# Queries first, scores ahead of states, set 2 held back, and identity matmuls in TensorE's first waits

## The chip, the cores and the metric

The kernel runs on one core of one Trainium2 chip. The metric is the device time of one execution in microseconds (us), as the median of several runs. An execution's profile has a span, from the first to the last instruction, and the execution's own time beside it.

## The reference

Decayed linear attention feeds a two-layer feed-forward block. B, H, S, D are 4, 8, 768, 64; the feed-forward widths are 512 and 2048.

```
Dmask = where(rel >= 0, lam ** rel, 0)            # rel = i - j within a block of 64
for each block b of 64 positions:
    intra = ((q_b @ k_b.T) * Dmask) @ v_b
    inter = (q_b * lam ** (pos + 1)) @ kv_state
    attn[b] = intra + inter
    kv_state = lam ** 64 * kv_state + (k_b * lam ** (63 - pos)).T @ v_b
x = attn with heads side by side                  # 3072 x 512
h = x @ w_in                                      # 3072 x 2048
out = (h * sigmoid(h)) @ w_out                    # 3072 x 512
```

## The kernel before

Positions are taken in units of 128, 24 units in all. Two units make a set, and there are 12 sets. The first four hold units 0 and 1 of one batch entry, interleaved by position; the other eight hold one unit of two batch entries. A set is loaded as three float32 tiles `raw` (k, q, v; `load_set`, L349 and L351), 0.5 MB each, on SyncE's (SP's) DMA queue, in the order k, q, v.

For one set: k and q are cast to bfloat16 (`kq`, L313 on ScalarE = ACT, L315 on VectorE = DVE); both are transposed (`kqT`), on TensorE (PE) by matmuls with the identity `ident` (L442) for the first four sets and by a DMA (L622) for the others; v is multiplied by a decay (`vd`). TensorE then makes the states (`d_ps`, L463 or L647) from k and `vd`, the scores (`st_ps`, L514 or L657) from `kqT`, and, after VectorE has masked the scores to `st`, the outputs (`x_ps`, L538 or L679), to which the carried state `xe` is added by a second group of matmuls (L543 or L687). `y`, `xf` and `yf` are the steps from `d_ps` to the next `xe`. VectorE multiplies `x_ps` by the queries' decay `lam_xe` while it moves it to `xt`, the transposed activations. `lam_xe` is made at the start on ACT from the integer row `row_i`.

The feed-forward part takes `xt` in groups: four of 256 columns (one for each of the first sets), then four of 512. `product1` (L830) multiplies by w_in into `h_ps`, ACT applies silu into `g` (L839), and `product2_plain` (L861) multiplies the first eight units by w_out into `o_ps`. The sixteen other units go through seven products for eight (a Strassen-Winograd scheme; `product2`, L1072, with sums `s` and `wsum`), and so does the last group's first product (`product1_spared`, L944). Results leave through `osb`.

The weights are loaded and cast to bfloat16 by GpSimd's (POOL's) DMA queue in quarters of 0.5 MB as they lie on chip (`load_w`; w_in is i0 to i3, w_out o0 to o3). `SEQUENCE` gives the order of sets and weights. Between them stand gates: `gated` lets POOL copy one element of a loaded `raw` tile, so that the weight loads behind it in POOL's queue are not issued before that load has landed. In before each gate waits for the k of the set named last.

The order of every engine is written out by `Planner.order`, a list scheduler: each task has a key, the engines that it may run on with an estimated time on each, its inputs and its buffers from small pools; the planner plays the tasks through and emits them in that order. TensorE runs its matmuls in program order, so one that waits holds all behind it.

Of the kernel before, what the change touches and what calls it, by code (L numbers as in the profile page):

```python
# [37 lines left out]
class Planner:  # L38

    LAT = {"PE": 0.23, "ACT": 0.06, "DVE": 0.06, "POOL": 0.08, "SP": 0.0}  # L40
    BEGIN = {"PE": 0.8, "ACT": 8.3, "DVE": 4.5, "POOL": 4.7, "SP": 0.8}
    FIRST, LAST, AHEAD = {"SP": 1.9, "ACT": 1.15, "POOL": 2.5}, 1.0, 0.75

    def __init__(self, pools):
        self.pools = {n: list(range(c)) for n, c in pools.items()}
        self.tasks = []

    def add(self, key, on, fn, deps=(), bufs=(), nbytes=0, kind=None, prior=(), late=0.0):
        key = key if isinstance(key, tuple) else (key,)
        t = Task(key, on, fn, deps, list(bufs) + [b.with_ for b in bufs if b.with_], nbytes, kind, prior, late)  # L50
        for b in t.bufs:
            b.left += 1
        self.tasks.append(t)
        return t

    def order(self):
# [14 lines left out]
        seq = 0  # L71
# [48 lines left out]
        while len(out) < len(self.tasks):  # L120
# [9 lines left out]
            for e in free:  # L130
# [8 lines left out]
                while ready[e]:  # L139
# [12 lines left out]
                    mine = now + t.on[e]  # L152
                    if any(max(free[o], now) + d < mine - 1e-9 for o, d in t.on.items() if o != e):
                        kept.append((key, i, t))
                        continue
# [4 lines left out]
                if took is None:  # L160
                    continue
# [5 lines left out]
                free[e] = now + t.on[e]  # L167
                heapq.heappush(events, free[e])
# [20 lines left out]
def kernel(  # L189
# [28 lines left out]
    SEQUENCE = "s0 i0 s1 i1 i2 s2 i3 o0 s3 o1 o2 o3 s4"  # L218
    POOLS = dict(bank=8, ra=3, rb=6, kq=3, kqT=3, vd=3, st=3, xe=6, xf=3, y=2, yf=2,
                 xt2=2, xt4=2, g=18, s=12, m=3, osb=3, one=3, two=4, att=6)  # L220
    BY_POOL, IN_BY_POOL, PLAIN, SPARED = (4,), (), 8, 1
    EARLY, PACE = 1.0, 1.0
    EAGER, CALM, ON = 8.0, 1.0, 6.0
# [36 lines left out]
    row_i = const.tile([128, U], mybir.dt.int32, name="row_i")  # L260
    nc.gpsimd.iota(row_i, pattern=[[1, U]], base=-64, channel_multiplier=0)
# [20 lines left out]
    pose_2 = const.tile([128, 2], F32, name="pose_2")  # L282
    for a in range(2):
        nc.vector.tensor_scalar(pose_2[:, a:a + 1], iota_2, -1.0, 64.0 - a, op0=AL.mult, op1=AL.add)
    pose = const.tile([128, 1], F32, name="pose")
    nc.vector.tensor_scalar(pose, iota_p, -1.0, 64.0, op0=AL.mult, op1=AL.add)
    row = const.tile([128, U], F32, name="row")
    nc.vector.tensor_copy(row, row_i)
# [6 lines left out]
    lam_v = const.tile([128, H], F32, name="lam_v")  # L295
    lam_xe = const.tile([128, NP, U], F32, name="lam_xe")
    lam_be = const.tile([128, NP], F32, name="lam_be")
    lam_v2 = const.tile([128, H, 2], F32, name="lam_v2")
    for a in range(2):
        nc.scalar.activation(lam_v2[:, :, a], log_all, AF.Exp, scale=pose_2[:, a:a + 1])  # L300
    nc.scalar.activation(lam_v, log_all, AF.Exp, scale=pose[:, 0:1])
    for a in range(NP):
        nc.scalar.activation(lam_xe[:, a, :], row, AF.Exp, scale=log_lam[:, a:a + 1])
# [26 lines left out]
    def gated(key, load, i, tile):  # L330
        pool_task(add(key, {"POOL": 0.15}, lambda e: nc.gpsimd.tensor_copy(gate[:, i:i + 1], tile()), deps=load,  # L331
                      prior=pool_last[-1:]))
# [3 lines left out]
    raw = {}  # L336

    def load_set(key, si):
        n, b = sets[si][0]
        nb = 2  # L340
        rs = [Buf("ra" if si in (0, 3) else "rb") for _ in range(3)]
# [4 lines left out]
        def go(e, i):  # L346
            if n < PAIRED:
                tile_of(rs[i], [128, H, 2, 64], F32, "raw")
                nc.sync.dma_start(out=rs[i].tile.rearrange("p h e d -> p h (e d)"), in_=x[i])  # L349
            else:  # L350
                nc.sync.dma_start(out=tile_of(rs[i], [128, 2 * H, 64], F32, "raw"), in_=x[i])  # L351

        for i in range(3):
            ts.append([add((key, i), {"SP": 0.55}, lambda e, i=i: go(e, i), bufs=[rs[i]], nbytes=0.524,
                           kind=WIDE if n < PAIRED else SMALL, late=0.3 if si < FRESH else 3.0)])
        raw[si] = rs, ts
# [3 lines left out]
    def load_w(key, what, j):  # L360
        def go(e):
            if what == "i":
                cs = slice(512 * j, 512 * j + 512)
                nc.gpsimd.dma_start(out=w_in_bf[:, :, cs], in_=w_in_r[:, :, cs])
            else:
# [3 lines left out]
        wload[what, j] = pool_task(add((key, 0), {"POOL": 0.8}, go, [], [], 1.0486,  # L369
                                       LARGE, prior=pool_last[-1:], late=1.0))  # L370

    last, unit = None, None
    for m, x in enumerate(SEQUENCE.split() + [f"s{i}" for i in range(len(sets))]):
        j = int(x[1:])
        if x[0] == "s":
            if j not in raw:
                load_set(m - 100, j)
                unit = j
        else:
            if last != unit:  # L380
                rs, loads = raw[unit]
                gated((m - 100, -1), loads[0], unit, lambda b=rs[0]: b.tile[:, 0, 0, 0:1] if len(b.tile.shape) == 4 else b.tile[:, 0, 0:1])
                last = unit
            load_w(m - 100, x[0], j)
# [25 lines left out]
    def key_of(si):  # L410
        u = rank[sets[si][0]]
        return u - 4.0 if sets[si][0][0] == 0 else u - LEAD

    def prepare_2(o, rs, lk, lq, lv):
# [5 lines left out]
        def cast(e, i, a):  # L420
            copy(e, o.kq_of()[:, i, :, a], rs[i].tile[:, :, a, :].rearrange("p (m h) d -> p m h d", h=2))

        o.ck = [[add((s - 1.0, i), {"DVE": 0.43, "ACT": 0.63}, lambda e, i=i, a=a: cast(e, i, a), deps=(lk, lq)[i],
                     bufs=[rs[i], o.kq]) for a in range(2)] for i in range(2)]
# [7 lines left out]
        o.cv = [add((s - 0.8, 0), {"DVE": 0.7}, lambda e, a=a: scale_v(e, a), deps=lv, bufs=[rs[2], o.vd]) for a in range(2)]  # L432
# [19 lines left out]
    def first_2(o):  # L452
# [13 lines left out]
        td = add((s - 0.6, 0), {"PE": 0.45}, states, deps=o.cv + o.ck[0], bufs=d_ps + [o.kq, o.vd])  # L466
        after("b", td)
# [13 lines left out]
        def blocks(xe, i, src, t, buf):  # L481
            def go(e, r):
                if xe.tile is None:
# [6 lines left out]
        t0 = add((s - 0.9, 3), {"DVE": 0.42}, lambda e: tt(e, small(xf), d_ps[0].tile, rate, AL.mult), deps=[td], bufs=[d_ps[0], xf])  # L490
        o.xe_ready = blocks(o.xe_in, 0, lambda: xf.tile, t0, xf)
        t1 = add((s - 0.9, 4), {"DVE": 0.42}, lambda e: tt(e, small(y), d_ps[1].tile, xf.tile, AL.add), deps=[td, t0],
                 bufs=[d_ps[1], xf, y])
        t2 = add((s - 0.9, 5), {"DVE": 0.42, "POOL": 0.7}, lambda e: tt(e, xf_of(), y.tile, rate, AL.mult), deps=[t1], bufs=[y, xf_n])
        xf_t.append(t2)
        xe_t += blocks(xe_n, b0 % 2, xf_of, t2, xf_n)

# [6 lines left out]
        o.st_of = st_of  # L504
        deps = [t for t in o.turned]
        o.masked = []
        for g in range(2):
# [11 lines left out]
            for p in range(2):  # L519
# [5 lines left out]
                o.masked.append(add((s - 0.9, 0), {"DVE": 0.69}, mask, deps=[ts], bufs=[st_ps[g][p], o.st2[p]]))  # L525
        after("m", o.masked)

    def second_2(o):
# [21 lines left out]
        for c in range(2):  # L550
            def evac(e, c=c):
                tl = tile_of(xt[gi], [128, KI, 256], BF16, "xt")
                dst = tl[:, :, 128 * c:128 * c + 128].rearrange("p m (c e) -> p m e c", e=2)
                tt(e, dst, x_ps[c].tile, lam_xe.rearrange("p m (c e) -> p m e c", e=2), AL.mult)

            xt_done[gi].append(add((s - 0.9, 6), {"DVE": 0.7}, evac, deps=[(t0, t1)[c]], bufs=[x_ps[c], xt[gi]]))

    def prepare(si):
# [7 lines left out]
        o.kq, o.kqT, o.vd, o.st = Buf("kq"), Buf("kqT"), Buf("vd"), Buf("st")  # L566
# [6 lines left out]
        def kq_of():  # L573
            return tile_of(o.kq, [128, nb, 2, NP, 2, 64], BF16, "kq")

        def kqT_of():
            return tile_of(o.kqT, [128, nb, 2, NP, U], BF16, "kqT")
# [9 lines left out]
        def cast(e, j, i):  # L587
            src = rs[i].tile[:, j * H:j * H + H, :].rearrange("p (m h) d -> p m h d", h=2)
            dst = kq_of()[:, j, i]
            copy(e, dst, src)  # L590

        ck = [[add((s - 1.0, i), {"DVE": 0.43, "ACT": 0.63}, lambda e, j=j, i=i: cast(e, j, i), deps=(lk, lq)[i],
                   bufs=[rs[i], o.kq]) for i in range(2)] for j in range(nb)]
        after("k", [t for ts in ck for t in ts])
# [4 lines left out]
        cv = [add((s - 0.8, 0), {"DVE": 0.7} if si < FRESH else {"POOL": 1.25, "DVE": 0.7}, lambda e, j=j: scale_v(e, j),  # L599
# [5 lines left out]
        if si < TURNED:  # L605
            for j in range(nb):
                bank = Bank(fills=False)

                def turn(e, j=j, bank=bank):
                    t = tile_of(bank, [128, 2, NP, U], BF16, "tr")  # L610
                    for i in range(2):
                        for m in range(NP):
                            nc.tensor.transpose(t[:, i, m, :], kq_of()[:, j, i, m], ident)

                tr = add((s - 0.7, j), {"PE": 0.46}, turn, deps=ck[j], bufs=[bank, o.kq])
                for i in range(2):
                    o.turned.append(add((s - 1.0, 2), {"DVE": 0.43, "ACT": 0.6},
                                        lambda e, j=j, i=i, bank=bank: copy(e, kqT_of()[:, j, i], bank.tile[:, i]),
                                        deps=[tr], bufs=[bank, o.kqT]))
        else:  # L620
            def dma_turn(e):
                nc.sync.dma_start_transpose(kqT_of().rearrange("p b i m s -> p (b i m) s"),  # L622
                                            kq_of().rearrange("p b i m h d -> p (b i m h d)"))
# [4 lines left out]
    def first_part(o):  # L628
# [12 lines left out]
        def states(e):  # L641
            for j in range(nb):
                for m in range(NP):
                    for c in halves_of_d:
                        r = halves[c]
                        for p, rp in enumerate(halves):
                            nc.tensor.matmul(d_of(c)[rp, j, m, :], lhsT=o.kq_of()[r, j, 0, m, p, :],  # L647
# [3 lines left out]
        def scores(e):  # L651
            for j in range(nb):
                for m in range(NP):
                    for p, rp in enumerate(halves):
                        t = tile_of(st_ps[p], [128, nb, NP, 64], F32, "st_ps")
                        for c, r in enumerate(halves):
                            nc.tensor.matmul(t[r, j, m, :], lhsT=o.kqT_of()[rp, j, 0, m, r], rhs=o.kqT_of()[rp, j, 1, m, r],  # L657
# [6 lines left out]
    def second_part(o):  # L664
# [18 lines left out]
        def inter(e):  # L683
            for c in range(2):
                for j in range(nb):
                    for m in range(NP):
                        nc.tensor.matmul(x_of(c)[:, j, m, :], lhsT=o.xe[c].tile[:, (bs[0] + j) % 2, m, :],  # L687
                                         rhs=o.kqT_of()[:, j, 1, m, halves[c]],
# [484 lines left out]
```

## Time and profile before

| | before |
|---|---|
| median of 3 runs | 207.87 us (207.69 to 208.84) |
| profiled execution | 207.82 us |
| its span | 206.1 us |
| TensorE busy | 187.0 us (91%), 2445 matmuls |
| VectorE busy | 134.8 us (65%) |
| ScalarE busy | 107.4 us (52%) |
| GpSimd busy | 52.4 us (25%) |
| mean DMA rate | 165 GB/s |

A line such as "L830 PE MATMUL h_ps<-xt,w_in_bf" names the line of the kernel, the engine, the operation and the tiles; "xt" is a tile's name, "x16" a count. All copies stand under L313, L315 or L317 and all two-input operations under L320, by engine, so there the tile names tell the step. An arrow in brackets names what ended the engine's idle time.

### The profile page before, as it was taken

The numbers are of one execution on the slowest core, as the hardware profiler recorded it, in microseconds if no ns is written. First come the engines' busy times: TensorE is split into PE (matmuls) and PEld (weight loads), VectorE is DVE, ScalarE is ACT, GpSimd is POOL, SyncE is SP. The second block draws the span as 40 slices with busy tenths as digits, with TensorE's granted clock in tenths as the row PEclk, the third lists the DMA queues.
The fourth block names the chain that finished last, engine by engine and source line by source line (L and its number), as shares of the span: only waits on it lengthen the run. The fifth ranks groups of instructions, "written<-read, shape, count | busy, mean of one in ns | idle before, by whom it ended". The sixth has DMA issues, their size and how long they took to land.

```text
span 206.1 us, 5719 instructions
## 1 busy us (share of the span) xinstructions
PE 187.0 (91%) x2445; PEld 132.9 (64%) x2464; DVE 134.8 (65%) x249; ACT 107.4 (52%) x195; POOL 52.4 (25%) x76
## 2 busy tenths in 40 slices
PE   0459399999999999999999999998999999999993
PEld 0347288786667565544578648474675778888882
DVE  6488632767950467716989953999758995665411
ACT  3637267874336453375734492745615453766420
POOL 7231400401130111222565013346003221222200
PEclk9999889999999999999999999999999999999999
DMA  3999999999999999999999999905101110102213
GB/s 99 292 253 260 228 222 265 235 199 214 228 238 249 156 216 231 238 219 195 263 213 234 203 213 240 244 7 117 39 3 54 51 54 0 54 0 102 88 52 118
DMA packets 88617, 33.92 MB, mean 165 GB/s; under 512 B 67088, under 2 KB 87568, under 8 KB 88592
## 3 DMA queue, kind: packets, MB, share of 16 engines
q1 hardware_dynamic: 79232, 23.60, 57.3%
q0 software_dynamic: 4224, 4.19, 12.2%
q10 hardware_dynamic: 5136, 5.77, 8.7%
q8 instruction: 19, 0.31, 0.7%
q14 instruction: 6, 0.05, 0.1%
HBM read 27.27 MB, written 6.29 MB: 163 GB/s over the span
## 4 chain that ended last, share of the span: by engine, by line
PE 82%; DMA 8%; DVE 7%; issue 1%; ACT 0%; POOL 0%; POOLq 0%; DVEq 0%
PE h_ps L830 31%; PE o_ps L1072 22%; PE o_ps L861 13%; PE h_ps L944 6%; DMA w_in_bf<-in_moe_w_in_dram 5%; DMA raw<-in_k_dram 3%; PE x_ps L687 2%; DVE s L320 2%; PE tr L442 2%; DVE g L320 1%; PE d_ps L647 1%; PE x_ps L679 1%; PE st_ps L657 1%; PE x_ps L538 1%; DVE kq L315 1%
## 5 line engine op out<-in xcount | busy, mean ns | idle before, releaser
L830 PE MATMUL h_ps<-xt,w_in_bf 128*128 128x256 bf16 (+1 forms) x439 | 75.7, 322 | 4.7 <-DMA w_in_bf<-in_moe_w_in_dram 3.3
L839 ACT ACTIVATE g<-h_ps 128x512 bf16<-128x512 f32 x80 | 47.1, 594 | 45.7 <-PE h_ps L830 45.0
L830 PEld LDWEIGHTS <-w_in_bf 128*128 128x128 bf16 x448 | 43.7, 99 | 30.1 <-DMA w_in_bf<-in_moe_w_in_dram 3.5
L861 PE MATMUL o_ps<-w_out_bf,g 128*128 128x512 bf16 x118 | 29.7, 379 | 0.6 <-issue 0.2
L320 POOL TENSOR_TENSOR s<-g,s 128x512 bf16<-128x512 bf16 x16 | 19.0, 1188 | 43.1 <-DVE s L320 26.8
L320 DVE TENSOR_TENSOR st<-st_ps,tri 128x512 bf16<-128x512 f32 x32 | 20.5, 681 | 11.2 <-PE st_ps L657 11.2
L1072 PEld LDWEIGHTS <-g 128*128 128x128 bf16 x256 | 24.9, 98 | 4.4 <-ACT g L839 0.3
L320 DVE TENSOR_TENSOR xt<-x_ps,lam_xe 128x512 bf16<-128x512 f32 x24 | 15.9, 699 | 15.2 <-PE x_ps L687 9.5
L1072 PEld LDWEIGHTS <-s 128*128 128x128 bf16 x192 | 18.7, 98 | 2.6
L861 PEld LDWEIGHTS <-g 128*128 128x128 bf16 x128 | 12.1, 98 | 12.0
L320 POOL TENSOR_TENSOR vd<-raw,lam_v 128x512 bf16<-128x512 f32 x10 | 13.3, 1334 | 25.1 <-DMA raw<-in_v_dram 19.7
L313 ACT ACTIVATE kq<-raw 128x512 bf16<-128x512 f32 x27 | 16.2, 621 | 2.1 <-DMA raw<-in_q_dram 1.6
L320 DVE TENSOR_TENSOR osb<-o_ps,m 128x512 f32<-128x512 f32 (+1 forms) x15 | 8.7, 583 | 10.9 <-ACT m L313 6.8
L1072 PE MATMUL o_ps<-wsum,g 128*128 128x256 bf16 x128 | 15.3, 272 | 0.0
L1072 PE MATMUL o_ps<-w_out_bf,s 128*128 128x256 bf16 x128 | 15.3, 273 | 0.0
L442 PE MATMUL tr<-ident,kq 128*128 128x128 bf16 x64 | 7.0, 260 | 8.8 <-POOL gate L331 6.9
L1072 PE MATMUL o_ps<-w_out_bf,g 128*128 128x256 bf16 x128 | 15.0, 273 | 0.0
L320 DVE TENSOR_TENSOR s<-g 128x512 bf16<-128x512 bf16 x16 | 8.2, 510 | 10.4 <-ACT g L839 6.6
L313 ACT ACTIVATE m<-o_ps 128x512 f32<-128x512 f32 (+1 forms) x14 | 7.0, 503 | 11.4 <-PE o_ps L1072 11.4
L320 DVE TENSOR_TENSOR vd<-raw,lam_v 128x512 bf16<-128x512 f32 x14 | 9.2, 681 | 5.0 <-DMA raw<-in_v_dram 5.0
L313 ACT ACTIVATE osb<-o_ps 128x512 f32<-128x512 f32 (+1 forms) x12 | 6.7, 562 | 10.4 <-PE o_ps L861 6.5
L315 DVE CAST kq<-raw 128x512 bf16<-128x512 f32 x21 | 9.1, 451 | 3.8 <-DMA raw<-in_k_dram 2.0
(88 smaller groups left out, 215.1 us busy)
## 6 DMA issues: line engine op xcount, KB each, us to landing
raw<-in_k_dram SPq DMA_DIRECT2D x12, 512.0 KB, 8.2
raw<-in_q_dram SPq DMA_DIRECT2D x12, 512.0 KB, 8.5
raw<-in_v_dram SPq DMA_DIRECT2D x12, 512.0 KB, 8.0
out_dram<-osb ACTq DMA_DIRECT2D x20, 256.0 KB, 3.6
w_in_bf<-in_moe_w_in_dram POOLq DMA_DIRECT2D x4, 512.0 KB, 10.0
w_out_bf<-in_moe_w_out_dram POOLq DMA_DIRECT2D x4, 512.0 KB, 11.7
out_dram<-osb ACTq DMA_DIRECT2D x4, 128.0 KB, 1.7
out_dram<-osb SPq DMA_DIRECT2D x4, 128.0 KB, 1.7
```

Source lines behind the costliest of these rows:

```text
L313: nc.scalar.activation(o, i, AF.Copy)
L315: nc.vector.tensor_copy(o, i)
L320: (nc.vector if e == "DVE" else nc.gpsimd).tensor_tensor(o, a, b, op=op)
L442: nc.tensor.transpose(t[:, m, a], o.kq_of()[:, i, m, a], ident)
L538: nc.tensor.matmul(t[rh, m], lhsT=o.vd_of()[r, 2 * m + h, a, :], rhs=o.st_of(h)[r, m, a], start=m == 0 and a == 0, stop=True, skip_group_c ...
L647: nc.tensor.matmul(d_of(c)[rp, j, m, :], lhsT=o.kq_of()[r, j, 0, m, p, :], rhs=o.vd_of()[r, j, 2 * m + p, :], start=j == 0 and m == 0, sto ...
L687: nc.tensor.matmul(x_of(c)[:, j, m, :], lhsT=o.xe[c].tile[:, (bs[0] + j) % 2, m, :], rhs=o.kqT_of()[:, j, 1, m, halves[c]], start=False, s ...
L830: nc.tensor.matmul(t[:, j, :], lhsT=w_in_bf[:, ko, 128 * (m1 + j):128 * (m1 + j) + 128], rhs=xt[gi].tile[:, ko, :], start=(ko == 0), stop= ...
L839: nc.scalar.activation(t[:, half * per:half * per + per], bank.tile, AF.Silu)
L861: nc.tensor.matmul(t, lhsT=g.tile[:, j, 128 * gp:128 * gp + 128], rhs=w_out_bf[:, ko, :], start=(ko == 0), stop=(ko == KO - 1))
L944: nc.tensor.matmul(t[:, j, :], lhsT=W[w]()[:, k2, f:f + 128], rhs=X(r)[:, k2, :], start=first and j == 0 and k2 == 0, stop=True, skip_grou ...
L1072: nc.tensor.matmul(t[:, i_, :], lhsT=src(j)[:, k2, 128 * r:128 * r + 128], rhs=W[w]()[:, 2 * j + k2, :], start=first and i_ == 0 and j == ...
```

## The change

- **Loads.** The first four sets are loaded as q, k, v. `SEQUENCE` names with "@" the load behind which an item stands: i0 behind set 0's v, i1 (with i2, i3, o0 after it) behind set 1's k, and set 2 behind set 1's v, by a one-element DMA that stands in SP's queue and waits for that load. o1 to o3 stand behind set 2's k.
- **The queries' decay** moves from the evacuation of `x_ps` to the cast of q, which becomes a multiply (`lam_q`, `lam_q2`) on VectorE, for the later sets also on POOL. The evacuation to `xt` becomes a plain copy on ACT or VectorE. `row_i`, `row` and `lam_xe` go; k and q of a later set lie as two halves of `kq`.
- **Order in a set.** In sets 0 and 1 the scores and their masks stand ahead of the states and what follows from them (`rest`).
- **Filler.** Where TensorE has nothing ready, between 2.2 and 26 us of the planner's clock, the planner puts in four matmuls of `ident` with itself, into one PSUM bank that it holds for this; from 9.6 on only after 0.6 us without work. The program has 68 such matmuls: 40 ahead of the first transposes, and then 8, 4, 8, 4 and 4.
- **The spared group.** `product1_spared` copies its first product into the second's PSUM bank on ACT and adds onto it there, in place of four adds on VectorE, and applies silu to halves.
- **Planner and pools.** Other estimates, a bias of 0.2 against VectorE, other pools, and earlier w_in sums. These decide the order of all engines anew.

The core of the diff:

```diff
+    WARM, COLD, REST = (2.2, 26.0), 9.6, 0.6
...
-    SEQUENCE = "s0 i0 s1 i1 i2 s2 i3 o0 s3 o1 o2 o3 s4"
+    SEQUENCE = "s0 i0@0.2 s1 i1@1.0 i2 i3 o0 s2@1.2 o1 o2 o3 s3 s4"
...
+    QUERIES = (0, 1, 2, 3)
+    SCORED, SOON, VD_ON, HALVED = (0, 1), 3, {"DVE": 0.7, "POOL": 1.25}, 0
...
-        for i in range(3):
+        for i in (1, 0, 2) if si in QUERIES else range(3):
...
+                held = [add((m - 100, -1), {"SP": 0.15}, lambda e, g=gates, tile=tile: nc.sync.dma_start(
+                    out=gate[0:1, g:g + 1], in_=tile()[0:1]), deps=loads[i], bufs=[rs[i]], prior=sp_last[-1:])]
...
+            if i:
+                tt(e, dst, src, lam_q[:, :, None].to_broadcast([128, H, 64]), AL.mult)
+            else:
+                copy(e, dst, src)
...
-                tt(e, dst, x_ps[c].tile, lam_xe.rearrange("p m (c e) -> p m e c", e=2), AL.mult)
+                copy(e, dst, x_ps[c].tile)
...
+        if o.si in SCORED:
+            rest()
...
+                        free[e] = rested = now + 0.44 if now < self.COLD else now + 0.22
+                        heapq.heappush(events, free[e])
+                        out.append((now, len(out), e, self.filler(fill)))
...
+            for i in range(4):
+                nc.tensor.matmul(t[:, i, :], lhsT=ident, rhs=ident, start=i == 0, stop=True, skip_group_check=True)
```

More of the change, by code (lines that the diff above doesn't have):

```diff
@@ L119, in order @@
                 arm(t)
-        while len(out) < len(self.tasks):
+        fillers, fill, rested = 0, None, 0.0
+        while len(out) < len(self.tasks) + fillers:
             if not events:
@@ L328, in pool_task, with gated @@
         return t
-    def gated(key, load, i, tile):
-        pool_task(add(key, {"POOL": 0.15}, lambda e: nc.gpsimd.tensor_copy(gate[:, i:i + 1], tile()), deps=load,
+    def gated(key, load, i, tile, buf):
+        pool_task(add(key, {"POOL": 0.15}, lambda e: nc.gpsimd.tensor_copy(gate[:, i:i + 1], tile()), deps=load, bufs=[buf],
                       prior=pool_last[-1:]))
@@ L336 @@
     raw = {}
+    sp_last = []
     def load_set(key, si):
@@ L340, in load_set @@
         nb = 2
-        rs = [Buf("ra" if si in (0, 3) else "rb") for _ in range(3)]
+        rs = [Buf("rb") if si >= CASTING and i == 0 else None if si >= CASTING and i == 1 else Buf("ra" if si in (0, 3) else "rb")
+              for i in range(3)]
         ts = []
@@ L367, in go @@
                 nc.gpsimd.dma_start(out=w_out_bf[:, ks, :], in_=w_out_r[:, ks, :])
-        wload[what, j] = pool_task(add((key, 0), {"POOL": 0.8}, go, [], [], 1.0486,
-                                       LARGE, prior=pool_last[-1:], late=1.0))
+        t = pool_task(add((key, 0), {"POOL": 0.8}, go, [], [], 0.5243 if part else 1.0486,
+                          HALF if part else LARGE, prior=pool_last[-1:], late=1.0))
+        wload.setdefault((what, j), []).append(t)
+        for h in ("a", "b") if not part else part:
+            wload[what, j, h] = t
     last, unit = None, None
+    gates = 0
     for m, x in enumerate(SEQUENCE.split() + [f"s{i}" for i in range(len(sets))]):
-        j = int(x[1:])
+        x, _, behind = x.partition("@")
+        j, part = int(x[1:].rstrip("ab")), x[-1] if x[-1] in "ab" else ""
+        if x[0] == "s" and j in raw:
+            continue
+        if x[0] == "i" or x[0] == "o":
+            if last != unit or behind:
+                behind = behind or f"{unit}.0"
+                last = unit
+        if behind:
+            u, i = map(int, behind.split("."))
+            rs, loads = raw[u]
+            tile = lambda b=rs[i]: b.tile[:, 0, 0, 0:1] if len(b.tile.shape) == 4 else b.tile[:, 0, 0:1]
+            if x[0] == "s":
+                held = [add((m - 100, -1), {"SP": 0.15}, lambda e, g=gates, tile=tile: nc.sync.dma_start(
+                    out=gate[0:1, g:g + 1], in_=tile()[0:1]), deps=loads[i], bufs=[rs[i]], prior=sp_last[-1:])]
+            else:
+                gated((m - 100, -1), loads[i], gates, tile, rs[i])
+            gates += 1
         if x[0] == "s":
-            if j not in raw:
-                load_set(m - 100, j)
-                unit = j
-        else:
[L380 to L384, printed above, removed]
+            load_set(m - 100, j)
+            if behind:
+                raw[j][1][QUERIES.count(j)][0].prior += held
+            unit = j
+        else:
+            load_w(m - 100, x[0], j, part)
     groups = GROUPS
@@ L420, in cast @@
         def cast(e, i, a):
-            copy(e, o.kq_of()[:, i, :, a], rs[i].tile[:, :, a, :].rearrange("p (m h) d -> p m h d", h=2))
-        o.ck = [[add((s - 1.0, i), {"DVE": 0.43, "ACT": 0.63}, lambda e, i=i, a=a: cast(e, i, a), deps=(lk, lq)[i],
-                     bufs=[rs[i], o.kq]) for a in range(2)] for i in range(2)]
+            src = rs[i].tile[:, :, a, :].rearrange("p (m h) d -> p m h d", h=2)
+            if i:
+                rate = lam_q2[:, :, a].rearrange("p (m h) -> p m h", h=2)
+                tt(e, o.kq_of()[:, i, :, a], src, rate[:, :, :, None].to_broadcast([128, NP, 2, 64]), AL.mult)
+            else:
+                copy(e, o.kq_of()[:, i, :, a], src)
+        o.ck = [[add((s - 1.0, i), {"DVE": 0.7} if i else {"DVE": 0.45, "ACT": 0.63}, lambda e, i=i, a=a: cast(e, i, a),
+                     deps=(lk, lq)[i], bufs=[rs[i], o.kq]) for a in range(2)] for i in range(2)]
         after("k", [t for ts in o.ck for t in ts])
@@ L504, in first_2, with rest @@
         o.st_of = st_of
+        def rest():
+            td = add((s - 0.6, 0), {"PE": 0.45}, states, deps=o.cv + o.ck[0], bufs=d_ps + [o.kq, o.vd])
+            after("b", td)
+            t0 = add((s - 0.9, SOON), {"DVE": 0.42}, lambda e: tt(e, small(xf), d_ps[0].tile, rate, AL.mult), deps=[td], bufs=[d_ps[0], xf])
+            o.xe_ready = blocks(o.xe_in, 0, lambda: xf.tile, t0, xf)
+            t1 = add((s - 0.9, 4), {"DVE": 0.42}, lambda e: tt(e, small(y), d_ps[1].tile, xf.tile, AL.add), deps=[td, t0],
+                     bufs=[d_ps[1], xf, y])
+            t2 = add((s - 0.9, 5), {"DVE": 0.42, "POOL": 0.7}, lambda e: tt(e, xf_of(), y.tile, rate, AL.mult), deps=[t1], bufs=[y, xf_n])
+            xf_t.append(t2)
+            xe_t.extend(blocks(xe_n, b0 % 2, xf_of, t2, xf_n))
+        if o.si not in SCORED:
+            rest()
         deps = [t for t in o.turned]
@@ L779, in evac @@
                     src = o.x_of(c)[:, js[0]:js[0] + nj]
[L780 to L786 removed]
+                    copy(e, dst, src)
+                xt_done[gi].append(add((o.s - 0.9, 6), {"ACT": 0.17 + 0.215 * nj, "DVE": 0.15 + 0.27 * nj}, evac, deps=[t], bufs=[o.x_ps[c], xt[gi]]))
     for si in range(len(sets)):
@@ L852, in product2_plain @@
         row = b * S + n * U
-        bank, two, two2, osb = Buf("bank"), Buf("two"), Buf("two"), Buf("osb")
+        bank, osb = Buf("bank"), Buf("osb")
+        twos = [Buf("two") for _ in range(2 if u < OPEN else POOLS["two"] // 2)]
         s = 4.0 + u
```

248 lines of the change are left out of this document (140 added, 108 removed).

## The prediction

> **What bounds the kernel now.** I read the page first, then the chain of waits in order of time, the waits of TensorE alone after 28 us, the timeline of the first 30 us, and one-microsecond windows. On the page, TensorE (PE) is busy in nearly every slice from the eighth on, and not in the first six.
>
> ```profile
> span 206.1 us, 5719 instructions
> PE   0459399999999999999999999998999999999993
> PEclk9999889999999999999999999999999999999999
> ```
>
> From 28 us to 203 us only two waits of TensorE are listed, 0.9 us together:
>
> ```profile
> PE h_ps L830 <- DVE xt L320: 0.7, 1, 0.7
> PE o_ps L861 <- issue: 0.2, 1, 0.2
> ```
>
> So this is a TensorE-bound kernel with a poor opening. The chain of waits shows where the opening goes; its columns are start, length, what:
>
> ```profile
> 13.15 0.39 POOL xe L317
> 13.54 0.05 issue
> 13.59 0.12 POOL gate L331
> 13.71 10.23 DMA w_in_bf<-in_moe_w_in_dram
> ...
> 23.99 3.41 PE h_ps L830 x16
> 27.40 0.70 PE x_ps L538 x21
> ```
>
> The second quarter of w_in is issued only at 13.71, because its gate stands behind a state cast in GpSimd's (POOL's) queue, though the gate's own load had landed at 11.7. It lands at 23.94, and TensorE, in program order, stands before it. The timeline and windows (TensorE's busy time, then the granted clock) show that wait and a second loss, the clock:
>
> ```profile
> 16.79 0.91 PE L442 MATMUL tr<-ident,kq 128*128 128x128 bf16 x8
> 17.92 1.91 PE L830 MATMUL h_ps<-xt,w_in_bf 128*128 128x256 bf16 x16 [0.22 <-DVE xt L320]
> ...
> 23.99 3.41 PE L830 MATMUL h_ps<-xt,w_in_bf 128*128 128x256 bf16 x16 [3.34 <-DMA w_in_bf<-in_moe_w_in_dram]
> ```
> ```profile
> 22.00:23.00 1.00, 0.00 (x0) 0.00 (x0) 1.00 (x2) 0.26 (x1) 0.98 (x2) 1.00 1.20 218
> ...
> 25.00:26.00 1.00, 1.00 (x7) 0.69 (x5) 0.00 (x0) 0.27 (x1) 0.00 (x0) 0.50 1.17 290
> ```
>
> Sixteen h_ps matmuls that take 1.75 us elsewhere took 3.41 us after the idle stretch, at a granted clock of 0.50.
>
> **The sum's frame.** TensorE's real work is the same in both programs. From the chain's rows at full speed: 256 h_ps of 256 columns at 109 ns (16 in 1.75) 28.0; 192 of 512 columns at 215 ns (4 in 0.86) 41.3; 112 h_ps of the spared group at 109 ns 12.2; 128 o_ps of 512 columns at 217 ns 27.7; 448 of 256 at 109 ns 48.9; 64 transposes at 56 ns (8 in 0.45) 3.6; four first sets at 0.38 + 0.45 + 0.57 + 0.33, 6.9; eight later ones, 12.5. Sum 181.1 us. In before, the work done when TensorE starts at 24.0 and stops waiting is 32 transposes 1.8, d_ps 0.76, st_ps 0.9, one x_ps pair 0.9, 16 h_ps 1.75: 6.1 us. The slow clock then costs 3.41 - 1.75 + 0.70 - 0.57 = 1.8. So the opening loses 24.0 - 6.1 + 1.8 = 19.7 us, and 19.7 + 181.1 = 200.8; TensorE ends at 202.5, so 1.7 us are lost later. The tail is 206.1 - 202.5 = 3.6, and 207.82 - 206.1 = 1.7 lies outside the span. The profiled execution's 207.82 us is the median, 207.87, within 0.05. What the change is worth is what it makes of the 19.7.
>
> **Loads.** Landings in before (issue plus time to landing): k0 6.46, q0 8.2, v0 10.0, k1 11.7, 1.75 us apart; with weights flowing, k2 19.7, q2 25.4, v2 31.1, k3 36.8, 5.7 apart; weights w_in 14.9 (issued 7.1), 23.9, 27.7, 31.3, some 3.7 apart back to back. A weight quarter thus takes most of the rate and a set's load crawls. Swapping q and k costs nothing: either is 0.5 MB. After: q0 6.46, k0 8.2, v0 10.0, q1 11.7. The first weight gate now waits for v0, so w_in 0 is issued at 10.6 instead of 7.1 and lands at 18.4 by the same 7.8 us; k1 is out of its way at 13.5, v1 is caught for its second part, 17.1. The second gate (k1, 13.5) has nothing ahead of it in POOL's queue but that issue, so three w_in and one w_out issues go at 13.9 to 16.9 (0.75 each), back to back behind w_in 0. SP's new one-element copy waits for v1 and holds all later loads to 17.1, so w_in 1 has two microseconds alone: 21.5, then 25.1, 28.7, w_out 0 32.3. Estimates, from these spacings.
>
> **Set 0.** The q multiply on VectorE (DVE) is the vd row's shape, 0.68 instead of a 0.42 cast, but runs 6.46 to 7.75, before k0 lands: hidden. Transposes end at 8.3 and 9.4, copies at 10.1 (ACT shares them once the table load is over at 8.3; four lam_xe of 0.38 became three of about 0.28). Scores now precede states, so they no longer wait for vd: 10.1 to 10.6 against 12.2 to 13.3. vd 10.0 to 11.3, four masks in 2.48 to 13.8, outs at 13.85 against 15.39.
>
> **Set 1.** VectorE then has y, k1 half, y, q1 half, xf, q1 half: 13.8 to 16.8, so q1's transposes come at 16.8 although q1 landed at 11.7; copies to 18.3, scores 18.35, masks 18.85 to 21.3, outs 21.35, carried part (y, cast) 22.2 to 22.5. Set 0's evacuations are copies on ACT, done at 17.7, and its 16 h_ps on w_in 0 (18.4) run between, hidden. So set 1 is complete at 22.5, against 28.4, and w_in 1 has landed: the work done by then is 7.0 (6.1 plus 0.9). Lost: 22.5 - 7.0 = 15.5. From there the program alternates set 0 and set 1, so that each quarter feeds 32 matmuls, 3.5 us, about the 3.6 us at which quarters land: needed at 26.0 and 29.5, there at 25.1 and 28.7. Gain 19.7 - 15.5 = 4.2.
>
> **Held set 2.** q2 27.8, k2 33.0, v2 34.8, q3 36.6, k3 41.1 (crawling until w_out 0 is in, then fast until w_out 1, gated by k2, flows near 36.5). TensorE wants their transposes at 31.3, 34.1, 38.5, 41.3 and d_ps 2 at 37.1. Only k3 is late, with its 0.6 cast: take 0.4, bounds 0 and 9.5 (below).
>
> **Filler.** Forty identity matmuls stand first, at 0.117 (the slow transposes, 8 in 0.94) to 0.056 each: 4.7 to 2.2 us from ident's end at 1.4, over by 6.1 before the first transposes at 7.8. The other 28 come in fours and eights, 0.22 to 0.94, in gaps of 0.6 and more on the dates above. Cost taken: none; bounds 0 to 2 if dates move together (five groups of some 0.4). Their held bank leaves seven; no TensorE wait on a bank is listed.
>
> **The rest.** VectorE loses 24 xt multiplies (15.9) and 11 casts (5.0), gains 18 q multiplies (12.3) and 8 copies (5.5): -3.1. ACT loses 13 casts (8.1), gains 16 copies (9.6): +1.5. POOL gains 6 q multiplies, 1.04 to 2.81 each. The spared group swaps four adds for copies into PSUM. None is on TensorE's path after 28 us; by the same work count the later sets' d_ps stand within 3.5 us of their old times (66.9 against 68.5, 146.3 against 148.8), so their loads need not be faster. Later losses stay 1.7, bounds 0 and 5.
>
> **Sum.** 15.5 + 181.1 + 1.7 + 0.4 = 198.7; + 3.6 + 1.7 = 204.0; with parts of the 1.7 as likely to shrink as grow, forecast 203.9.
>
> **Rivals.** *The clock falls again.* In before, TensorE was some 40 to 60% busy from 7 to 17 us and still slow (0.91 for 8 transposes at 16.79). With filler it is about 44% busy from 10 to 18. If that is too little, set 1's transposes and scores double (+0.9) and the first full stretch is slow, 1.8 as at 24 us, partly inside waits: +2.0, 205.9. Against it: the drop in before came after 3.3 us with nothing at all, and no gap after is over 1.7. The Trainium skill (TensorE: Matmul & The Clock Gate, Part 1) says that about 3.4 us of activity frees the clock and an idle window as long throttles it; before's drop agrees, and by that the filler keeps speed; how busy a window must be it doesn't say.
>
> *Loads of sets 2 and 3 too late, slower.* If the weights never pause, all loads crawl at 5.7: q2 27.8, k2 33.5, v2 39.2, q3 44.9, k3 50.6, and TensorE stands in order before set 3's transposes: 51.2 - 41.3 = 9.9, 0.4 of it counted: 213.4. It decides from k3 landing near 46. Against: w_out 1 is gated by k2, which makes the pause.
>
> *Helpers late.* VectorE was busy 4.3 to 5.0 of each 5 us from 100 to 120; a POOL vd took 2.81 at 55.87 beside VectorE's sums, casts and vd, against 1.04 at its shortest, and six more such operations come. If q casts reach the DMA transposes 1 us late in four of eight sets, the gain is gone: 207.9. The Trainium skill (SBUF — State Buffer, Who interferes with whom) says one of the two waits whole; the 2.81 agrees.
>
> **Chances.** Forecast 0.60 (201.8 to 205), clock 0.15, helpers 0.13, loads 0.12. 201.8 is the sum with all 0.4 + 1.7 lost later gone; 207.0 leaves out the loads and half of the helpers, 0.18. About 0.5%, 1.0 us, is what a measurement can tell: faster (under 206.8) 0.60 + 0.15 + 0.05, same 0.08, slower 0.12.
>
> **What would show it.** Right: full-speed h_ps (1.75 for 16) from 19 us, w_in 1 issued near 14, continuous work from about 22.5, span near 202.2. Wrong: a granted clock under 0.9 between 10 and 26, a TensorE wait over 1 us on set 3's transposes near 41, or new waits on xt or kqT after 60.

## The result

The changed kernel takes 215.45 us (median of six runs) beside 208.07 for the kernel before on the same chip: 1.036 times as long, 95% interval 1.031 to 1.041. The forecast was 203.9 and a gain of 4.2; it lost 7.4. The profiled execution took 215.72 us with a span of 214.0.

### The profile page after: what moved, and what is told of

It is laid out like the page before. It is cut to its first block, busy times and chain, and to the rows that moved or that the text cites. A ratio compares the mean times of both kernels' runs of the same rounds, so it can differ in the third digit from the quotient of the medians.

```text
span 214.0 us, 5888 instructions
## 1 busy us (share of the span) xinstructions
PE 198.0 (93%) x2532; PEld 140.8 (66%) x2532; DVE 134.7 (63%) x237; ACT 114.4 (53%) x207; POOL 56.8 (27%) x75
## 4 chain that ended last, share of the span: by engine, by line
PE 75%; DVE 15%; ACT 4%; issue 3%; DMA 2%; ACTq 0%; DVEq 0%
PE h_ps L900 30%; PE o_ps L1148 21%; PE o_ps L935 9%; PE h_ps L1018 5%; DVE st L348 3%; DVE kq L348 2%; DVE vd L348 2%; DMA lam_sb<-in_lam_dram 2%; PE tr L507 2%; PE x_ps L761 2%; DVE xsum L348 1%; DVE y L348 1%; PE d_ps L721 1%; DVE osb L348 1%; DVE g L348 1%
## 5 line engine op out<-in xcount | busy, mean ns | idle before, releaser
L348 POOL TENSOR_TENSOR s<-g,s 128x512 bf16<-128x512 bf16 x16 | 19.5, 1219 | 67.1 <-DVE s L348 52.3
L348 DVE TENSOR_TENSOR st<-st_ps,tri 128x512 bf16<-128x512 f32 x32 | 20.2, 683 | 19.3 <-PE st_ps L731 19.3
L935 PE MATMUL o_ps<-w_out_bf,g 128*128 128x512 bf16 x128 | 30.8, 379 | 0.0
L1148 PEld LDWEIGHTS <-s 128*128 128x128 bf16 x192 | 19.4, 102 | 4.8 <-issue 1.6
L348 POOL TENSOR_TENSOR vd<-raw,lam_v 128x512 bf16<-128x512 f32 x11 | 13.0, 1183 | 22.0 <-DMA raw<-in_v_dram 11.7
L348 DVE TENSOR_TENSOR osb<-o_ps,m 128x512 f32<-128x512 f32 (+1 forms) x15 | 8.6, 581 | 15.2 <-ACT m L341 11.1
L1148 PE MATMUL o_ps<-w_out_bf,s 128*128 128x256 bf16 x128 | 16.9, 290 | 1.3 <-DVE osb L348 1.3
L348 DVE TENSOR_TENSOR kq<-raw,lam_q 128x512 bf16<-128x512 f32 x18 | 14.6, 825 | 3.1 <-ACT lam_q L331 1.9
L348 DVE TENSOR_TENSOR s<-g 128x512 bf16<-128x512 bf16 x16 | 10.5, 658 | 6.1 <-ACT g L912 3.4
L341 ACT ACTIVATE m<-o_ps 128x512 f32<-128x512 f32 (+1 forms) x14 | 7.3, 519 | 11.8 <-PE o_ps L1148 8.7
L341 ACT ACTIVATE osb<-o_ps 128x512 f32<-128x512 f32 (+1 forms) x13 | 7.3, 565 | 11.4 <-PE o_ps L935 6.6
L341 ACT ACTIVATE xt<-x_ps 128x512 bf16<-128x512 f32 x16 | 10.1, 652 | 5.8 <-PE x_ps L608 3.0
L348 POOL TENSOR_TENSOR kq<-raw,lam_q 128x512 bf16<-128x512 f32 x6 | 8.3, 1385 | 15.0 <-PE x_ps L761 5.9
L343 DVE COPY kqT<-tr 128x512 bf16<-128x512 bf16 x7 | 3.0, 423 | 12.7 <-ACT kqT L341 6.7
```

What stands on the lines that cost most here:

```text
L341: nc.scalar.activation(o, i, AF.Copy)
L343: nc.vector.tensor_copy(o, i)
L348: (nc.vector if e == "DVE" else nc.gpsimd).tensor_tensor(o, a, b, op=op)
L935: nc.tensor.matmul(t, lhsT=g.tile[:, j, 128 * gp:128 * gp + 128], rhs=w_out_bf[:, ko, :], start=(ko == 0), stop=(ko == KO - 1))
L1148: nc.tensor.matmul(t[:, i_, :], lhsT=src(j)[:, k2, 128 * r:128 * r + 128], rhs=W[w]()[:, 2 * j + k2, :], start=first and i_ == 0 and j == ...
```

## The profile after

In the changed kernel the copies stand under L341 (ACT), L343 (VectorE) and L345 (GpSimd), and the two-input operations under L348 (L353 for VectorE's in e13 below).

The page first. TensorE is busy from the first slice on, yet it keeps dropping to 8 and once to 6 in the middle, where before had a single 8, and the clock drops twice in the opening and once more in the slices at 145 to 155 us.

```profile
span 214.0 us, 5888 instructions
PE   7577999999989999989998899996999989999993
PEclk9785699999999999999999999998899999999998
```

The waits of TensorE alone after 28 us (what was waited for; us in total, times, longest) were two, 0.9 us, in before:

```profile
PE o_ps L1148 <- DVE osb L348: 1.3, 2, 0.7
PE d_ps L721 <- DVE vd L348: 1.2, 1, 1.2
PE x_ps L608 <- DVE st L348: 0.9, 2, 0.5
PE h_ps L1018 <- ACT m L341: 0.7, 1, 0.7
PE o_ps L1148 <- ACT m L341: 0.7, 1, 0.7
PE h_ps L900 <- ACT osb L341: 0.7, 1, 0.7
PE tr L507 <- DVE y L348: 0.2, 1, 0.2
```

They are 5.7 us, all on VectorE or on ACT's copies. None is on a load, and the wait for w_in 1 in the opening (3.34 us in before) is gone. The timeline of TensorE in the opening (start, length; in brackets the idle time before):

```profile
18.87 0.93 PE L507 MATMUL tr<-ident,kq 128*128 128x128 bf16 x7 [1.33 <-DVE kq L348]
...
20.48 1.10 PE L582 MATMUL st_ps<-kqT 64*64 64x128 bf16 x32 [0.26 <-ACT kqT L341]
21.51 1.89 PE L900 MATMUL h_ps<-xt,w_in_bf 128*128 128x256 bf16 x8
...
25.95 0.40 PE L613 MATMUL x_ps<-kqT,xe 128*128 128x128 bf16 x4
26.18 3.98 PE L900 MATMUL h_ps<-xt,w_in_bf 128*128 128x256 bf16 x35
```

Eight h_ps take 1.89 us where 1.05 is full speed. From 20.48 to 42 us the timeline shows no wait of TensorE, but up to about 25 it runs slowly: the work that the forecast had done at 22.5 is done at 26.2. The one-microsecond windows give the clock (the column before the last two):

```profile
16.00:17.00 1.00, 1.00 (x12) 1.00 (x10) 1.00 (x2) 0.97 (x3) 1.00 (x2) 0.50 1.20 185
...
22.00:23.00 1.00, 1.00 (x7) 0.68 (x5) 1.00 (x3) 0.00 (x0) 0.00 (x0) 0.50 1.20 218
...
25.00:26.00 1.00, 1.00 (x37) 0.69 (x36) 0.42 (x1) 0.52 (x1) 0.39 (x1) 1.00 1.17 208
```

It is 0.50 from about 8 to 11 and from 14.7 to 24.9 us. Last, the timeline of VectorE and GpSimd, at two places:

```profile
15.82 1.20 DVE L348 TENSOR_TENSOR kq<-raw,lam_q 128x512 bf16<-128x512 f32 x1
16.95 1.26 DVE L348 TENSOR_TENSOR xf<-y,lam_be 128x256 f32<-128x256 f32 x1
...
57.07 2.66 DVE L348 TENSOR_TENSOR wsum<-wsum,w_out_bf 128x1024 bf16<-128x1024 bf16 x1
57.14 1.04 POOL L348 TENSOR_TENSOR kq<-raw,lam_q 128x512 bf16<-128x512 f32 x1
...
58.14 1.04 POOL L348 TENSOR_TENSOR vd<-raw,lam_v 128x512 bf16<-128x512 f32 x1
```

The sum of weights takes 0.68 alone and 2.66 here: 0.68 plus the two GpSimd operations that run beside it. At 15.82 and 16.95 two operations that take 0.68 and 0.42 alone take 1.36 more together, about the 1.29 of GpSimd's vd (recorded from 16.63 to 17.92; the first of them starts 0.8 ahead of that, and GpSimd's spans in a profile are rough). This holds the second half of q1, and so the transposes at 18.87. In e13 below, where this vd leaves its values out, they take 0.68 and 0.41.

To place the loss I take TensorE's time less the full-speed work that it has done (the prediction's frame), at the d_ps of a set (set 2's stand at 37.10 in before and 41.12 in after, with 17.5 and 21.8 us of such work done; 181.1 are done at the end):

| us lost at | set 2 | end of TensorE | after set 2 |
|---|---|---|---|
| before | 19.6 | 21.3 | 1.7 |
| predicted after | 15.5 | 17.6 | 2.1 |
| after | 19.3 | 29.2 | 9.9 |

Against the forecast, 3.8 us are lost in the opening and 7.8 behind it. Of the 9.9, 5.7 are the listed waits; 1.6 more is a slow stretch (16 o_ps in 3.52 at 147.91, 1.91 elsewhere) behind the waits of 144 to 148 us. The profiles of e1 and e2 have nearly the same waits and not this stretch.

## The experiments

Two theories: (A) VectorE and GpSimd hinder each other, and the moved decay gives them more to meet on (36 two-input operations on GpSimd against 27, and 18 q multiplies on VectorE, which read SBUF, for 24 of x_ps, which read PSUM); (B) the clock, which the filler does not hold. A rival of both: (C) the planner's new order is poorer as such. Ratios are to before, with 95% intervals.

**The filler: e1, e2.**

```diff
-            for i in range(4):                # e1: one matmul in all, order kept
+            n = 4 if len(count) < 10 else 12  # e2: 84 in place of the 28 later ones
```

> The changed kernel with 67 of its 68 identity matmuls left out; every other instruction stands in the same order. Clock theory (the filler is too thin to hold TensorE's clock, which was 0.50 from 14.9 to 24.4 us with it): the opening is slow either way, so the time stays at 215 to 217, the first stretch of 80 h_ps starts within 1 us of 26.2, and the granted clock rises at the same place, 24 to 25 us. Rival, the filler does hold part of the opening: 217.5 or more. Rival, the filler itself stands in the way: 214 or less.

> The changed kernel with three times the identity matmuls in each group after the first forty (84 in place of 28), same order otherwise. Clock theory: the granted clock stays at 1.00 from 8 us on, set 1's scores take 0.5 instead of 1.1, the first 16 h_ps 1.75 instead of 3.4, the stretch of 80 h_ps starts near 23.5 instead of 26.2, and the time falls by 2 to 3 us to 212.5 to 213.5. Rival, VectorE's chain (q multiplies, masks) sets the opening and the clock costs nothing: 215 to 216, stretch at 25.5 or later.

e1: 215.2 us, 1.034 (1.028 to 1.041). e2: 213.1, 1.025 (1.017 to 1.034). The filler as written brings nothing and costs nothing; set 1's first eight h_ps took 1.89 without it too. A denser one holds the clock at 1.00 from 12 us on (eight h_ps in 1.05) and returns 2.3 us by the medians, though their intervals overlap. In e2's profile only 0.8 of it is gained in the opening (18.5 lost at set 2 for 19.3): from set 1's scores to the long stretch TensorE takes 4.56 us instead of 5.70, but the 24 identity matmuls ahead of set 0's second transposes move set 0's masks from 12.44 to 13.58. Another 1.6 is the slow stretch at 147.91, far from any filler. So B is real, and a small part of the loss.

**GpSimd's multiplies: e3, e4, e5.** e3 copies q where the change multiplies it, and so leaves the queries' decay out of the result; e4 keeps the v and q multiplies off GpSimd; e5 adds e2's filler to e4.

```diff
-                tt(e, dst, src, lam_q[:, :, None].to_broadcast([128, H, 64]), AL.mult)
+                copy(e, dst, src)                                          # e3
-    ... VD_ON, HALVED = (0, 1), 3, {"DVE": 0.7, "POOL": 1.25}, 0
+    ... VD_ON, HALVED = (0, 1), 3, {"DVE": 0.7}, 0                         # e4
-        ck = [[add((s - 1.0, i), {"DVE": 0.7, "POOL": 1.25} if i else ...
+        ck = [[add((s - 1.0, i), {"DVE": 0.7} if i else ...                # e4
```

> The changed kernel with q copied instead of multiplied by its decay, on the same engines in the same order; the queries' decay is left out of the result. Contention theory (a VectorE operation with two inputs in SBUF waits whole for a GpSimd multiply, and the other way round; q's multiplies now are of that kind on both engines): VectorE's q steps fall from 0.83 to 0.42 each (7 us of its time), the lengthened ones near them go, TensorE's waits after 28 us fall from 5.7 to 3 us or less and the time to 210 to 212. Rival, the planner's new order is what costs, not the length of q's steps: 214 to 215.5.

> The changed kernel with no multiplies of v or q on GpSimd: all on VectorE, order made anew by the planner. Contention theory: no q or v step on VectorE above 0.75, no 2.66 us w_out sum, and the time falls to 211 to 213 although VectorE gets 17 multiplies (11.6 us) more. Rival, VectorE's load is the bound where TensorE waits (4.9 of each 5 us from 100 to 115): 216 to 219.

> The changed kernel with both cures: no multiplies of v or q on GpSimd, and three times the identity matmuls after the first forty. If the clock in the opening and the waits between VectorE and GpSimd are separate losses, their gains of 2.3 and 5.5 us add: 215.4 - 7.8 = 207.6 (206.8 to 208.6). If both hit the same place (set 1's scores in the opening), the gains overlap and it stays at 209 to 210.

e3: 210.5, 1.012 (1.005 to 1.019). e4: 210.0, 1.010 (1.007 to 1.014): 5.5 us come back, although VectorE now does more; its q multiply falls from 0.825 to 0.681 us in the mean. e5: 210.2, 1.014 (1.009 to 1.019): the gains don't add. It lost 19.0 at set 2, e4 17.5; 24 identity matmuls ran 2.66 us ahead of set 0's second transposes, which likely is the reason, though e2 has them too (2.38). A holds, but e4 still lost 4.8 us after set 2.

**Parts of the change on before: e6 (loads), e7 (decay), e9 (filler), and before without GpSimd's v multiplies (e8) and without its sums too (e12).** Each is planned anew.

```diff
-    SEQUENCE = "s0 i0 s1 i1 i2 s2 i3 o0 s3 o1 o2 o3 s4"
+    SEQUENCE = "s0 i0@0.2 s1 i1@1.0 i2 i3 o0 s2@1.2 o1 o2 o3 s3 s4"       # e6, with SP's gate and q first
-                tt(e, dst, x_ps[c].tile, lam_xe.rearrange("p m (c e) -> p m e c", e=2), AL.mult)
+                copy(e, dst, x_ps[c].tile)                                # e7, with the q multiplies
-        cv = [add((s - 0.8, 0), {"DVE": 0.7} if si < FRESH else {"POOL": 1.25, "DVE": 0.7}, ...
+        cv = [add((s - 0.8, 0), {"DVE": 0.7}, ...                         # e8, e12
-    BY_POOL, IN_BY_POOL, PLAIN, SPARED = (4,), (), 8, 1
+    BY_POOL, IN_BY_POOL, PLAIN, SPARED = (), (), 8, 1                     # e12
```

> The kernel before with the change of the loads alone (q first, the gates as in the change, set 2 behind set 1's v), order made anew. If the loads are worth what the prediction gave them, and the later order does not suffer: 204 to 205. If the opening is set by VectorE's chain and a slow clock, as the changed kernel's profile has it: 206.5 to 208.5. If holding set 2 starves the later sets: 210 or more.

> The kernel before with the queries' decay moved to q's cast alone (multiplies on VectorE, for later sets also on GpSimd; xt copied on ACT or VectorE), order made anew. Contention theory: 18 or so two-input multiplies on VectorE and some on GpSimd lengthen each other, as in the changed kernel: 210 to 213. Rival, the move is neutral and the changed kernel's loss comes from elsewhere in it: 207 to 208.5.

> The kernel before with no multiplies of v on GpSimd (all 24 on VectorE), order made anew. Contention theory: the ten GpSimd multiplies cost before little, as few met a VectorE operation with two SBUF inputs: 207 to 208.2. Rival, VectorE is the bound in the middle and 10 more multiplies (6.8 us) show: 209 or more. If even before loses by the contention: 206 or less.

> Before with the filler alone: identity matmuls wherever the planner finds TensorE without work between 2.2 and 26 us; loads, decay and order in a set as before. Theory (the filler is too thin to hold the clock, and costs nothing): the long wait for w_in 1 stays, the clock behind it is again 0.50 or at best full, so between no change (207.9) and the 1.8 us that the slow matmuls cost in before (206.1). Rival (groups of identity matmuls stand ahead of real work and delay it): over 209.

> Before with neither v multiplies nor product sums on GpSimd. Theory (in before the contention is hidden: 0.9 us of waits after 28 us in all): no change, 207 to 208.5. Rival (VectorE has no room for them): over 209.

e6: 210.4, 1.014 (1.009 to 1.018); the opening lost 17.8 at set 2, 1.8 less than in before, and 6.1 were lost behind it. e7: 209.6, 1.011 (1.008 to 1.015). e8: 207.9, 1.001 (0.999 to 1.004). e9: 210.6, 1.013 (1.004 to 1.022), with waits on w_in (1.4 at 34.32), vd, xt and osb behind a first h_ps that was still slow (16 in 3.42): the rival's time, not by its mechanism. e12: 208.6, 1.005 (1.002 to 1.008). So taking GpSimd's work away gains before nothing, and each of the parts run alone costs about 1%; e6 and e9 lose late (6.1 and 5.2 us after set 2). That is what C would give, too.

**The last of GpSimd's work: e10, e14, e16; the planner's estimates: e11.** e10 is e4 with the product sums s off GpSimd; e14 the change with only those off; e16 is e10 with the state steps xf off too. e11 is e4 with before's LAT, OVERLAP, BEGIN and BIAS.

```diff
-    BY_POOL, IN_BY_POOL, PLAIN, SPARED = (4,), (), 8, 1
+    BY_POOL, IN_BY_POOL, PLAIN, SPARED = (), (), 8, 1                      # e10, e14, e16
-        ..., {"DVE": dcost, "POOL": 0.25 + w / 560}, lambda e: tt(e, xf_of(), y.tile, rate, AL.mult),
+        ..., {"DVE": dcost}, lambda e: tt(e, xf_of(), y.tile, rate, AL.mult),   # e16, the narrower xf alike
```

> The changed kernel without the v and q multiplies on GpSimd, as in e4 (210.0), and the product sums s that GpSimd made on VectorE too. Theory (GpSimd's two-input operations still stretch VectorE's sums, 1.26 and 1.37 for 0.41 us at 101 to 106 us in e4): 0.9 us saved some five times, of which a part is on TensorE's path: 208.5 to 209.5. Rival (VectorE is full in these stretches, and four more sums of 0.41 per product cost as much as they save): 210 or more.

> The changed kernel without the v and q multiplies on GpSimd, as in e4 (210.0), planned with the estimates of before (LAT, OVERLAP, BEGIN and no bias against VectorE). Theory (any new order loses 3 to 5 us after 60 us where VectorE has no slack at 100 to 115 and 135 to 145 us, whatever the estimates): 209 to 212. Rival (the new estimates make the poor late order): the losses after set 2 fall from 4.8 to the 1.7 of before, 207 or less.

> The changed kernel with the product sums s on VectorE alone; v and q multiplies still on GpSimd too. Theory (multiplies and sums each cost several us: 5.5 by e4, 3.0 between e4 and e10): 215.4 - 3 = about 212.5, 211 to 214. Rival (only freeing GpSimd of both helps, as the remaining kind meets VectorE just as often): 215.

> The kernel of e10 without the state steps xf on GpSimd either, so that GpSimd has no two-input operation at all. Theory (five xf of 1.66 us mean in e10 stretch VectorE and keep the next state waiting): 205.5 to 207. Rival (VectorE becomes too full at 135 to 145 us): 207.5 or more.

e10: 207.0, 0.9955 (0.9917 to 0.9992), the fastest version with a whole result: 8.5 us under the changed kernel and about 1 under the one before, by the medians. The second difference is at the edge of what the runs can tell. It loses 17.5 at set 2 and 2.2 behind it. Its waits of TensorE after 28 us, all of them:

```profile
PE d_ps L721 <- ACT g L912: 0.5, 1, 0.5
PE h_ps L900 <- ACT xt L341: 0.3, 1, 0.3
```

e14: 214.1, 1.033 (1.030 to 1.037): the sums alone matter little while the multiplies stay, less than the 3 us expected. e16: 208.5, 1.007 (1.004 to 1.010): the rest of GpSimd's work is better left there. e11: 210.7, 1.013 (1.005 to 1.021), no faster than e4: the old estimates don't mend the order. It loses 7.2 behind set 2, with 1.8 of waits on w_out, which e4 has not.

**The order kept: e13, e17.** All kernels above but e1 to e3 have an order of their own. e13 and e17 keep the change's. In them GpSimd's two-input operations fill their output with a constant and work out at most one column in 64 of it; the other values are left out.

```diff
+        if e == "POOL":
+            nc.gpsimd.memset(o, 0.125)
+            nc.gpsimd.memset(o[..., half], 0.125)        # e17 only
+            nc.gpsimd.tensor_tensor(o[c], a[c], b[c], op=op)
```

> The changed kernel in its own order on every engine; each two-input operation of GpSimd (v and q multiplies, product sums, xf) fills its output with a constant and computes one column in sixty-four of it, so those values are left out, and it waits for and releases the same things. Theory (the late losses come from GpSimd's operations, directly and by stretching VectorE's, not from the new order as such): most of the 9.9 us lost after set 1 goes, 207 to 209. Rival (the planner's new order is itself poorer, as in before with the new loads alone, 210.4): 211 or more.

> e13 again (the changed kernel's order; GpSimd's two-input operations leave their values out), but each with a second, half-size fill, so that GpSimd is occupied about as long as an undisturbed multiply or sum takes in the changed kernel: 0.52 + 0.31 + 0.3, about 1.1, against 1.04 to 1.2. Theory (it is VectorE and GpSimd hindering each other when both read two tiles of SBUF, not GpSimd's own length): as e13, 206 to 208. Rival (GpSimd's operations are late because each takes 1.1 us): 211 or more.

e13: 206.6, 0.996 (0.993 to 0.999). e17, with GpSimd occupied as long as by undisturbed operations: 206.8, 0.997 (0.994 to 1.000). Both lose 2.6 us after set 2, not 9.9. The waits of TensorE after 28 us fall from 5.7 to 1.2 us in e13:

```profile
PE o_ps L1153 <- ACT m L341: 0.7, 1, 0.7
PE h_ps L905 <- ACT xt L341: 0.3, 1, 0.3
PE tr L512 <- DVE y L353: 0.2, 1, 0.2
```

The page's first part in after, and then in e13:

```profile
PE 198.0 (93%) x2532; PEld 140.8 (66%) x2532; DVE 134.7 (63%) x237; ACT 114.4 (53%) x207; POOL 56.8 (27%) x75
```
```profile
PE 196.3 (95%) x2532; PEld 140.5 (68%) x2532; DVE 120.4 (58%) x237; ACT 114.0 (55%) x207; POOL 40.6 (20%) x111
```

VectorE's same 237 instructions take 14.3 us less. The groups by shape (count, busy time, mean ns) say which, in after and then in e13:

```profile
L348 DVE TENSOR_TENSOR st<-st_ps,tri 128x512 bf16<-128x512 f32 x32 | 20.2, 683 | 19.3 <-PE st_ps L731 19.3
L348 DVE TENSOR_TENSOR kq<-raw,lam_q 128x512 bf16<-128x512 f32 x18 | 14.6, 825 | 3.1 <-ACT lam_q L331 1.9 <-DMA raw<-in_q_dram 1.2
L348 DVE TENSOR_TENSOR s<-g 128x512 bf16<-128x512 bf16 x16 | 10.5, 658 | 6.1 <-ACT g L912 3.4 <-ACT g L1042 2.6
...
L348 DVE TENSOR_TENSOR wsum<-wsum,w_out_bf 128x1024 bf16<-128x1024 bf16 x2 | 3.3, 1670 | 0.0
```
```profile
L353 DVE TENSOR_TENSOR st<-st_ps,tri 128x512 bf16<-128x512 f32 x32 | 20.2, 680 | 19.5 <-PE st_ps L736 19.5
L353 DVE TENSOR_TENSOR kq<-raw,lam_q 128x512 bf16<-128x512 f32 x18 | 12.0, 682 | 4.3 <-DMA raw<-in_q_dram 2.4 <-ACT lam_q L331 1.9
...
L353 DVE TENSOR_TENSOR s<-g 128x512 bf16<-128x512 bf16 x16 | 6.7, 422 | 7.2 <-ACT g L917 4.6 <-ACT g L1047 2.6
...
L353 DVE TENSOR_TENSOR wsum<-wsum,w_out_bf 128x1024 bf16<-128x1024 bf16 x2 | 1.4, 682 | 0.0
```

Multiplies and sums with both inputs in SBUF shrink to their lone durations; the masks, with one input in PSUM, were never stretched. C falls for the changed kernel's late loss, and GpSimd's length falls too: it is the meeting of the two engines. The opening is another matter: e13 lost 18.6 at set 2 and e17 17.3.

**Filler and clock in e10: e15 (denser), e18 (none, order of e10).** Their edits are those of e2 and e1.

> The kernel of e10 (207.0: no multiplies and no sums on GpSimd) with the 12-matmul groups of e2 in place of the later groups of 4. Theory (the clock at half speed from 9 to 18.5 us still costs e10 some 1 to 2 us, but groups of 12 delay set 0, as in e5): 206 to 208, about no change from e10. Rival (a dense filler brings its 2.3 us of e2 here): 204.7.

> The kernel of e10 (207.0) in its own order with 67 of the 68 identity matmuls left out. Theory (too thin to hold the clock in e10 too, granted 0.50 from 9 to 18.5 us): no change, 206.3 to 207.7. Rival (the filler is what brings the clock back at 18.9 us in e10): slow first matmuls of h_ps, some 2 us more, 209.

e15: 207.6, 0.999 (0.997 to 1.002), e18: 207.9, 1.001 (0.998 to 1.004). e10's first eight h_ps ran in 1.05 us at 20.03; in e18:

```profile
20.11 1.89 PE L900 MATMUL h_ps<-xt,w_in_bf 128*128 128x256 bf16 x8
```

So in these profiles, with GpSimd out of the way, the written filler brings full speed back earlier, at 18.9 us against about 24, and is worth some 1 us (17.5 against 18.8 lost at set 2), more than I expected. The intervals touch, and e13 and e17 differ as much at set 2 with one TensorE program, so its size isn't settled.

## Why the prediction was wrong

- **Loads**: right. The first w_in quarter was issued at 10.59 (10.6), w_in 1 at 13.67 (13.9); the wait on it is gone, and no transposes of set 3 waited for a load. The rival of late loads is out.
- **Set 1**: failed. The step gave VectorE lone durations up to 16.8. Set 0's masks began at 12.44 instead of 11.3, GpSimd's vd added 1.36, and q1 was done at 18.8; set 1's scores began at 20.48 instead of 18.35. That is 2.1 of the 3.8 us. The rest came behind it, on a slow clock: from there to the long stretch it took 5.70 us, 4.15 by the forecast and 4.56 in e2, at full speed.
- **Filler and the clock rival**: "cost none" was right (e1). That the filler keeps speed was wrong. The rival's price of 2.0 is near the 2.3 that e2 returns, but by chance: only 0.8 of it is in the opening. The Trainium skill (TensorE: Matmul & The Clock Gate, Part 1) speaks of an idle window of some 3.4 us; here no gap between matmuls was over 1.9, and yet the clock was 0.50 for some ten. So the longest gap was the wrong thing to count.
- **The rest**: the term that sank the sum. "None is on TensorE's path after 28 us" was wrong, and "later losses stay 1.7" came out at 9.9. I balanced VectorE's busy time by lone durations, -3.1 us, and took its spare time as cover. The rival *helpers late* named the mechanism and had its row (2.81 at 55.87), but priced it at the gain, some 4, gave it 0.13, and looked for it at the q casts; the waits came on osb, vd, st and m, and none on kqT. It cost 8 to 9 us (215.45 less 206.6 by the medians, 8.3 by the ratios to before), of which I reckon 7.3 (9.9 less 2.6) behind set 2. The Trainium skill (SBUF — State Buffer, Who interferes with whom) says that one of the two waits whole; the 2.66 at 57.07 agrees. The prediction's own row, 2.81 for 1.04, should have been in the sum and not in a rival alone.
- **Tail**: right, 3.5 for 3.6.

Open stays why before with the loads alone or the decay alone loses late (e6, e7): e6's longest waits are again for VectorE (osb 1.8 and s 1.7 us), but their order was not held fixed, and e7's profiled execution (212.16) lies 2.5 over its median, so it can't place the loss. The order in a set, the spared group and the pools were not run alone. The gain in the opening is smaller than 4.2, and its size stays open: 2.1 in e10, 2.3 in e17, but 1.0 in e13, which has e17's order on every engine and a longer slow stretch.

## What to carry to other kernels

Before moving an elementwise step from the evacuation of PSUM to the cast of an SBUF tile, count which operations of VectorE and GpSimd will then meet with their inputs in SBUF, and price each meeting at the sum of both. When a replanned variant is slower, keep the order and take one engine's work away: that separates a poor order from a poor neighbour in one run.

## What the runs showed of the hardware

- GpSimd filling a tile for about 1.1 us beside VectorE left VectorE's multiplies at 0.68 (e17), while two GpSimd multiplies of 1.04 stretched a VectorE sum of 0.68 to 2.66. Fills are not free of it everywhere: the casts of k averaged 0.52 in e13 and 0.42 in the changed kernel; why is not settled.
- The granted clock of a window doesn't show every slow stretch. In e18 the window below reads 1.00 while the h_ps at 20.11 ran at half speed; durations decide.

```profile
20.00:21.00 1.00, 1.00 (x13) 0.64 (x6) 1.00 (x3) 0.00 (x0) 0.00 (x0) 1.00 1.20 216
```

- Identity matmuls in small groups, with gaps under 2 us, had the clock at 0.50 from 14.7 to 24.9 us in the changed kernel and from 8.7 to 18.9 in e10. With one and the same TensorE program it was at 0.50 from 14.1 to 24.3 in e13 and only from 19.7 to 23.1 in e17. So when it fell, and not only whether, decided what the filler was worth, and one profile doesn't tell it.
